# Another order of the work around cells 3 and 4 and the first weight pieces, in an mLSTM cell with an act-GCU feed-forward

## The chip, the cores and the metric

The kernel runs on one core of one Trainium2 chip. The time is device microseconds of that core, the median of several executions. A profile is one more execution, recorded by the hardware profiler.

## The reference

An mLSTM cell is run over four batches, eight heads, 768 time steps and 40 dimensions. Its output, as 3072 rows of 320, goes through a feed-forward block with a cosine gate.

```python
for t in range(S):                                   # S = 768
    m_new = max(f_gate[t] + m, i_gate[t])
    f_stab, i_stab = exp(f_gate[t] + m - m_new), exp(i_gate[t] - m_new)
    m = m_new
    C = f_stab * C + i_stab * outer(v[t], k[t])      # 40 x 40 for each head
    n = f_stab * n + i_stab * k[t]
    y[t] = sigmoid(o_gate[t]) * (C @ q[t]) / max(abs(n @ q[t]), 1)
x = y as (3072, 320)
h = x @ w_in                                         # 320 -> 2048
out = (h * cos(h)) @ w_out                           # 2048 -> 320
```

The two weight matrices arrive as float64 and are turned into float32 on the chip.

## The kernel before

Time is cut into six chunks of 128 steps. A *cell* is one chunk of one batch with its eight heads, numbered n = 4 * chunk + batch, so there are 24. Within a cell the recurrence becomes matrices: scores (k against q, `scores`, L492), times a decay matrix E (`weigh`, L498), times v (`values`, L508 for the first four cells, L518 to L527 later, where the state from earlier chunks is added with the scaled q, qG). The output is divided by a denominator and gated by sigmoid(o): `normalize` for cells 0 to 3, `denominators` and `divide` for later ones. `seam` holds cell n's last matmuls: for cells 0 to 3 the transposes of y into xT (px, L610 and L612), and for all the state's increment (pu, L619). `seam_out` brings the last dimensions into xL, for cells from 4 on by two DMAs issued on ScalarE's queue (L626). `state` adds the increment, `fade` decays the state before.

E is built from running maxima of the gates that go through DRAM (M_d), are loaded as broadcasts (L369), masked on GpSimd (`decay_exponents`, an affine select, L399) and exponentiated on ScalarE (`decay`, L413). The gates of chunk 0 are handled first; those of chunks 1 to 5 ("later gates") are worked out beside cells 0 to 3, then transposed on TensorE into a table (`gates_turn`, L275, with a product of a diagonal, L276) and copied to `tab` by ScalarE (`gates_keep`, L281 and L282).

The feed-forward of a chunk is done in eight steps f2, each with two 128-column blocks of w_in. `Up(c, f2)` issues the up-projection into two PSUM banks (tag "up", two banks in all): four 128x512 products with w_in_sb (L667) and two for the last 64 rows of x with w_in_l (L661). Then come `near` on ScalarE (rounding, L675), `rest` on VectorE (L678), `sin` on ScalarE (L683) and `gate` on VectorE (L687), which frees the banks. `down` multiplies by w_out (L699), in the first chunk one step behind: `down_slot(0, f2)` issues `down(0, f2 - 1)`.

The order of each engine's instructions is the order in which the code issues them (a manual schedule): `first_cells` (cells 0 to 3), `first_period` (cell 4 with chunk 0's steps 0 and 1), then `both_parts(c, b)`, two steps f2 = 2b and 2b + 1 with cell 4(c + 1) + b between them. TensorE's clock is kept up in the head by `warm`, matmuls on zeros (L920).

Weights come in pieces. `weights_in(f)` loads three pieces for the steps 2f and 2f + 1: two of w_in_sb (four DMAs each, L141) and one of w_in_l (four DMAs, L179). `weights_out(p)` loads the piece of w_out for step p (one DMA of 640 KB, L185). A piece is converted by `take_apart` (two operations on ScalarE, L153 and L155), `bound` (two on VectorE, L159 and L160) and `put_together` (one on VectorE, L166, and one on GpSimd, L167). The raw pieces lie in pools: `pb` has four buffers, for input pieces and also for cell 3's E; `pc` has three, for output pieces. `load_out(p)` loads output piece p + 3 as soon as piece p is converted. Nearly all loads are issued on SP's queue, in program order, each after the load before it on its semaphore has landed; a load whose buffer isn't free yet holds all loads behind it.

`clear_low` sets to zero the second set of buffers for q and k in blocks (GpSimd, L448), `turn_blocks` transposes q and k in 32x32 blocks on VectorE (L465), `turn_gate` the gate o (L470), `scale_q` and `weigh_k` are GpSimd products (L474, L418), `odd_values` a GpSimd copy of parts of v (L424). `sin_next` runs a sine on one element, so that ScalarE's table is loaded ahead of the next `sin`.

Of the kernel before, what the change touches and what calls it, by code (L numbers as in the profile page):

```python
# [29 lines left out]
def kernel(  # L30
# [239 lines left out]
    def gates_turn():  # L270
        pg = ps_o.tile([128, R, 2, BH], FP, name="pg", tag="o")
        pd = ps_o.tile([128, R - 1, BH], FP, name="pd", tag="o")
        for c in range(R):
            for j, src in enumerate((a1, eW)):
                nc.tensor.transpose(pg[:, c, j], src[:, c], ident[0:BH, 0:BH])  # L275
        nc.tensor.matmul(pd.rearrange("p c b -> p (c b)"), one.to_broadcast([BH, 128]), dd.rearrange("r c b -> r (c b)"),  # L276
                         start=True, stop=True)
        return pg, pd

    def gates_keep(pg, pd):  # L280
        nc.scalar.copy(out=tab[:, 1:NC, 0:2], in_=pg)  # L281
        nc.scalar.copy(out=tab[:, 1:R, 3], in_=pd)  # L282
# [261 lines left out]
    def divide(n):  # L544
        c, b = divmod(n, B)
        vt, dn = heads_of[n], dns[n]
        yt = p1.tile([128, 3, C], FP, name="yt", tag="yt")
        nc.vector.tensor_tensor(out=yt, in0=vt, in1=oTs[n], op=OP.mult)
        nc.vector.reciprocal(out=dn, in_=dn)
        db = p1.tile([128, 3, C], FP, name="db", tag="db")  # L550
        for i, mask in enumerate(([FROM0] * 32, [FROM1] * 32, [FROM0] * 16 + [FROM1] * 16)):
            nc.vector.stream_shuffle(out=db[:, i], in_=dn, mask=mask)
        if b == 0:
            new_x(c)

        nc.vector.tensor_tensor(out=xT[c][:, NK * b:NK * b + NK + 1], in0=yt, in1=db, op=OP.mult)
        ys[n] = xT[c][:, NK * b + NK]
# [364 lines left out]
    def first_cells():  # L922
        nc.vector.memset(nil, 0.0)
        gates_in()
        nc.scalar.copy(out=ident_b, in_=ident)
        load(0, "qk")
        later_gates_in()
        load(0, "v")
        load(1, "qk")
        load_o(0, (0, 1))  # L930
        load(1, "v")
        load(2, "qk")
        load_E(0)
        load_E(1)
        warm(12)
        wall_in(0, 0, pmu)
        wall_in(0, 1, psum_o())
        gates_first()
        gates_first_out()
        spread(0, 0)  # L940
        decay_exponents_half(0, 0)
        turn(0)
        turn_out(0, False)
        gates_sums()
        spread(0, 1)
        decay_exponents_half(0, 1)
        decay(0)
        weigh_k(0)
        load_E(2)
        load(2, "v")  # L950
        load_E(3)
        load_o(0, (2, 3))
        load(3)
        pieces.extend(weights_in(0))
        wall_in(1, 0, psum_o())
        wall_in(1, 1, psum_o())
        gates_less_sums()
        spread(1, 0)
        decay_exponents_half(1, 0)
        scores(0)  # L960
        gates_maxima()
        turn(1)
        weigh(0)
        sigmoid(0, slice(0, 2))
        turn_out(1, False)
        spread(1, 1)
        decay_exponents_half(1, 1)
        gates_exponents()
        decay(1)
        weigh_k(1)  # L970
        values(0)
        normalize(0)
        scores(1)
        gates_exp()
        turn(2)
        turn_out(2, False)
        warm(2)
        seam(0)
        weigh(1)
        seam_out(0)  # L980
        state(0)
        load_two(B, "qk")
        decay_exponents(2)
        gates_diagonal()
        decay(2)
        weigh_k(2)
        values(1)
        load_M(B)
        outs.append((0, weights_out(0)))
        normalize(1)  # L990
        scores(2)
        turn(3)
        sigmoid(0, slice(2, 4))
        seam(1)
        weigh(2)
        decay_exponents(3)
        turn_out(3)
        seam_out(1)
        values(2)
        decay(3)  # L1000
        weigh_k(3)
        state(1)
        normalize(2)
        scores(3)
        pg = gates_turn()
        warm(1)
        seam(2)
        weigh(3)
        to_float32(*pieces.pop(0))
        seam_out(2)  # L1010
        state(2)
        for piece in pieces[0:2]:
            take_apart(*piece)
        gates_keep(*pg)
        values(3)
        more = weights_in(1)
        pieces.append(next(more))
        load_G(B)
        load_two(B, "Kv")
        normalize(3)  # L1020
        bound(pieces[0][0])
        put_together(*pieces.pop(0))
        warm(3)
        seam(3)
        decay_exponents(B)
        seam_out(3)
        bound(pieces[0][0])
        put_together(*pieces.pop(0))
        pieces.extend(more)
        load_M(B + 1)  # L1030
        outs.append((1, weights_out(1)))
        load_o(1)
        outs.append((2, weights_out(2)))
        load_E(B + 2)
        low_dimensions(B)
        turn_blocks(B)
        state(3)
        decay(B)
        weigh_k(B)
        odd_values(B)  # L1040
        scale_q(B)

    spot = const.tile([1, 1], FP, name="spot")
    nc.gpsimd.memset(spot, 0.0)
# [14 lines left out]
    def first_period():  # L1059
        n = B  # L1060
        up = Up(0, 0)
        scores(n)
        warm(8, psum_o())
        for e in range(2):
            up.near(e)
        for e in range(2):
            up.rest(e)
        weigh(n)
        for e in range(2):
            up.sin(e)  # L1070
            up.gate(e)
        values(n)
        seam(n)
        p, piece = outs.pop(0)
        take_apart(*piece)
        take_apart(*pieces[0])
        bound(piece[0])
        put_together(*piece)
        load_out(p)
        bound(pieces[0][0])  # L1080
        put_together(*pieces.pop(0))
        decay_exponents(n + 1)
        denominators(n)
        for piece in pieces:
            take_apart(*piece)
        turn_blocks(n + 1, "k")
        up = Up(0, 1)
        for dst, bits in pieces:
            bound(dst)
            put_together(dst, bits)  # L1090
        pieces.clear()
        for e in range(2):
            up.near(e)
        for e in range(2):
            up.rest(e)
        for e in range(2):
            up.sin(e)
            up.gate(e)
        clear_low()
        fade(n)  # L1100
        down_slot(0, 1)
        sigmoid(1)
        turn_blocks(n + 1, "q")
        turn_gate(n)
        state(n)
        divide(n)
        decay(n + 1)
        p = next_out()
        seam_out(n)
        scale_q(n + 1)  # L1110
        weigh_k(n + 1)
        sin_next()
        pieces.extend(weights_in(2))
        load_two(n + 2)
        load_E(n + 3)
        load_out(p)

    def both_parts(c, b):

# [2 lines left out]
        for i in range(2):  # L1122
# [11 lines left out]
            if i == 0:  # L1134
                if cell:
                    weigh(n)
                    if n + 1 < N:
                        decay_exponents(n + 1)
                for e in range(2):
                    up.sin(e)  # L1140
                    up.gate(e)
                if c > 0:
                    sums(c, f2)
                if b == 0 and c == 1:
                    sigmoid(c + 1)

                if c == 0:
                    made = [pieces.pop(0) for _ in range(min(1, len(pieces)))]
                    p, piece = outs.pop(0)
                    made.append(piece)  # L1150
                    for dst, bits in made:
                        take_apart(dst, bits)
                    for dst, bits in made:
                        bound(dst)
                    for dst, bits in made:
                        put_together(dst, bits)
                    load_out(p)
                if cell and n + 1 < N:
                    decay(n + 1)
            else:  # L1160
                if cell:
                    seam_out(n)
                if cell:
                    state(n)
                for e in range(2):
                    up.sin(e)
                    up.gate(e)
                if c > 0:
                    sums(c, f2)
                if n == B + 1:  # L1170
                    low_dimensions(n + 1)
                if pieces:
                    to_float32(*pieces.pop(0))
                if cell and n + 1 < N:
                    if c > 0:
                        weigh_k(n + 1)
                    odd_values(n + 1)
# [84 lines left out]
```

## Time and profile before

| | us |
|---|---|
| median of 3 runs | 533.39 |
| lowest, highest | 532.88, 535.65 |
| the profiled execution | 535.21 |
| its span | 533.4 |
| TensorE busy | 516.5 (97%) |
| VectorE, ScalarE, GpSimd busy | 422.8, 285.5, 226.2 |
| mean granted TensorE clock | 0.981 |

The span runs from the first to the last instruction that the profile shows; 1.8 us lie around it. Times in the parts below count from the start of the span. A busy engine is one with an instruction in it; TensorE at half clock counts as busy all the same, so its busy time is read together with the granted clock.

### The profile page before, as it was taken

The page shows a single profiled execution, that of the slowest core. Times are in us where ns is not written, and L with a number is a line of the kernel's source. Part 1 is how long each engine was busy: PE and PEld are TensorE (multiplying, and loading weights), DVE is VectorE, ACT ScalarE, POOL GpSimd, SP SyncE. Part 2 cuts the span into 40 slices and gives each one's busy share as a digit, 9 for nine tenths or more (in the row PEclk, how much of TensorE's full clock was granted, in tenths as well). Part 3 has the DMA queues.
Part 4 walks back from the last instruction along what each step waited for, and adds up shares of the span by engine and source line. Part 5 has one row for each costly group of instructions (what it writes and reads, how often), then busy time and mean ns, then how long its engine had stood idle before and what let it go on. Part 6 is the DMA issues. An engine that isn't in the chain of part 4 may idle for free.

```text
span 533.4 us, 10501 instructions
## 1 busy us (share of the span) xinstructions
PE 516.5 (97%) x3844; PEld 350.2 (66%) x3844; DVE 422.8 (79%) x908; ACT 285.5 (54%) x546; POOL 226.2 (42%) x369
## 2 busy tenths in 40 slices
PE   7999879999999999999999999999999999999997
PEld 4875436556667757667767667767657767575666
DVE  5867978997888878898878898878898878664645
ACT  2877597757566537826527826526836522232230
POOL 7524644554577572632632632642422421222211
PEclk9977979999999999999999999999999999999999
DMA  9969869978949449229149229159220000010001
GB/s 138 219 194 195 229 173 198 224 123 243 183 120 189 46 124 178 66 83 188 32 124 163 53 87 188 29 129 170 37 88 7 2 5 6 1 50 1 0 1 49
DMA packets 99939, 57.81 MB, mean 108 GB/s; under 512 B 62304, under 2 KB 92608, under 8 KB 99888
## 3 DMA queue, kind: packets, MB, share of 16 engines
q1 hardware_dynamic: 96352, 55.48, 48.6%
q10 hardware_dynamic: 3392, 1.49, 1.3%
q8 instruction: 30, 0.49, 0.4%
q14 instruction: 21, 0.17, 0.1%
q0 software_dynamic: 144, 0.18, 0.1%
HBM read 51.71 MB, written 4.11 MB: 105 GB/s over the span
## 4 chain that ended last, share of the span: by engine, by line
PE 81%; DVE 5%; DMA 5%; SPq 3%; ACT 3%; POOL 2%; issue 1%; DVEq 0%; POOLq 0%; ACTq 0%
PE pup L667 28%; PE acc L848 24%; PE pup L661 8%; PE po L699 5%; PE late L848 3%; PE ps L492 3%; PE vt L527 2%; PE vt L518 2%; DMA bits<-in_moe_w_in_dram 2%; DMA o<-in_o_gate_dram 2%; PE pu L619 1%; SPq L141 1%; SPq L329 1%; DVE t L465 1%; DMA bits<-in_moe_w_out_dram 1%
## 5 line engine op out<-in xcount | busy, mean ns | idle before, releaser
L667 PE MATMUL pup<-xT,w_in_sb 128*128 128x512 f32 x384 | 178.7, 609 | 2.3 <-POOL qr L448 2.0
L675 ACT ACTIVATE n<-pup 128x512 int32<-128x512 f32 x96 | 53.9, 594 | 187.6 <-PE pup L661 133.8
L667 PEld LDWEIGHTS pup<-xT,w_in_sb 128*128 128x128 f32 x384 | 71.2, 194 | 90.1 <-issue 84.5
L678 DVE SCALAR_TENSOR_TENSOR n<-pup,n 128x512 f32<-128x512 f32 x96 | 63.1, 687 | 70.0 <-ACT n L675 68.5
L741 POOL TENSOR_TENSOR D<-g 128x128 f32<-128x128 f32 x40 | 19.8, 495 | 214.2 <-DVE g L687 214.2
L683 ACT ACTIVATE n<-n 128x512 f32<-128x512 f32 x96 | 57.7, 627 | 26.6 <-DVE n L678 19.0
L687 DVE SCALAR_TENSOR_TENSOR g<-pup,n 128x512 f32<-128x512 f32 x96 | 61.7, 684 | 3.9 <-ACT n L683 3.3
L848 PE MATMUL acc<-w_out_sb,g 128*128 128x160 f32 x320 | 59.0, 306 | 0.0
L848 PE MATMUL acc<-T,g 128*128 128x160 f32 x304 | 55.0, 301 | 0.0
L661 PE MATMUL pup<-xL,w_in_l 64*128 64x512 f32 x192 | 54.2, 642 | 0.0
L848 PEld LDWEIGHTS acc<-w_out_sb,g 128*128 128x128 f32 x320 | 47.7, 190 | 8.7 <-issue 7.2
L413 ACT ACTIVATE E<-E,tab 128x128 f32<-128x128 f32 x160 | 49.0, 389 | 0.3
L848 PEld LDWEIGHTS acc<-T,g 128*128 128x128 f32 x304 | 45.9, 191 | 1.8 <-issue 1.4
L699 PE MATMUL po<-w_out_sb,g 128*128 128x320 f32 x128 | 37.9, 451 | 3.4 <-POOL w_out_sb L167 3.4
L699 PEld LDWEIGHTS po<-w_out_sb,g 128*128 128x128 f32 x128 | 24.9, 197 | 15.5 <-POOL w_out_sb L167 3.6
L848 PE MATMUL acc<-T,S 128*128 128x160 f32 x160 | 34.8, 300 | 0.0
L492 PEld LDWEIGHTS ps<-t,t 40*128 40x128 f32 (+1 forms) x384 | 24.7, 188 | 12.3 <-DVE t L465 6.2
L498 DVE TENSOR_TENSOR E<-ps,E 128x512 f32<-128x512 f32 x48 | 30.7, 680 | 0.0
L661 PEld LDWEIGHTS pup<-xL,w_in_l 64*128 64x128 f32 x192 | 14.5, 185 | 22.9 <-issue 21.2
L848 PE MATMUL acc<-w_out_sb,S 128*128 128x160 f32 x160 | 28.8, 300 | 0.0
L1048 ACT ACT_TABLE_LOAD x22 | 28.2, 1283 | 0.9 <-DVE w_out_sb L160 0.5
L492 PE MATMUL ps<-t,t 40*128 40x128 f32 (+1 forms) x384 | 26.3, 276 | 1.2 <-DVE t L465 1.2
(189 smaller groups left out, 882.0 us busy)
## 6 DMA issues: line engine op xcount, KB each, us to landing
E<-M_d SPq DMA_DIRECT2D x22, 512.0 KB
qr<-in_q_dram SPq DMA_DIRECT2D x36, 160.0 KB
kr<-in_k_dram SPq DMA_DIRECT2D x36, 160.0 KB
bits<-in_moe_w_out_dram SPq DMA_DIRECT2D x8, 640.0 KB
G<-G_d SPq DMA_DIRECT2D x20, 256.0 KB
bits<-in_moe_w_in_dram SPq DMA_DIRECT2D x32, 128.0 KB
out_dram<-o_sb SPq DMA_DIRECT2D x23, 160.0 KB
ks<-in_k_dram SPq DMA_DIRECT2D x10, 320.0 KB
```

The source lines that it names most:

```text
L413: nc.scalar.activation(out=Es[n][:, h], in_=Es[n][:, h], func=AF.Exp, scale=-1.0, bias=tab[:, c, 0, g:g + 1])
L492: nc.tensor.matmul(ps[j][:, p], kT[r, p], qT[r, p], start=True, stop=True)
L498: nc.vector.tensor_tensor(out=w, in0=pss[n][j], in1=w, op=OP.mult)
L661: nc.tensor.matmul(pu, w_in_l[r, f2], xL[c][r].rearrange("p b t -> p (b t)"), start=ahead, stop=not ahead)
L667: nc.tensor.matmul(pu.rearrange("p (b t) -> p b t", b=B), w_in_sb[:, i, ts(2 * f2 + e, 128)], xT[c][:, i:NK * B:NK], start=(i == 0 and not ...
L675: nc.scalar.activation(out=self.n[e], in_=self.pu[e], func=AF.Copy, bias=0.25)
L678: nc.vector.scalar_tensor_tensor(out=self.n[e].bitcast(FP), in0=self.pu[e], scalar=0.25, in1=self.n[e], op0=OP.add, op1=OP.subtract)
L683: nc.scalar.activation(out=r, in_=r, func=AF.Sin, scale=TWO_PI_DOWN)
L687: nc.vector.scalar_tensor_tensor(out=g, in0=self.pu[e], scalar=TWO_PI, in1=self.n[e].bitcast(FP), op0=OP.mult, op1=OP.mult)
L699: nc.tensor.matmul(po[c][b], gs[c, f][:, ts(b, C)], w_out_sb[:, f], start=(f == 0), stop=(f == NF - 1))
L848: nc.tensor.matmul(a, lhs, rhs, start=start, stop=stop)
L1048: nc.scalar.activation(out=spot, in_=spot, func=AF.Sin)
```

## The change

In `first_cells`, the later gates' transposes move from behind cell 3's scores to behind its values, and the warming matmuls with them: one became two ahead of cell 2's seam, three became two behind the transposes. The copy of the table moves behind cell 3's `seam_out`, and `scale_q(B)` goes ahead of `weigh_k` and `odd_values`.

In `first_period`, all three pieces of the second input weights are taken apart before anything else, and cell 4's values are copied from PSUM to SBUF on ScalarE (`out_of_psum`, new). The transpose of k moves behind the second step's `rest`. The second output piece is taken apart ahead of the sigmoid and put together ahead of cell 4's division; its successor (piece 4) is therefore loaded ahead of `weights_in(2)`. Denominators, fade, state, mask and the clearing stand ahead of that conversion. Cell 4's `seam_out` moves into `both_parts(0, 1)`, behind that step's sines, and the prepared sine goes. `divide` of cell 4 multiplies in place.

```diff
     def divide(n):
...
-        yt = p1.tile([128, 3, C], FP, name="yt", tag="yt")
+        yt = vt if n == B else p1.tile([128, 3, C], FP, name="yt", tag="yt")
...
         scores(3)
-        pg = gates_turn()
-        warm(1)
+        warm(2)
         seam(2)
         weigh(3)
...
             take_apart(*piece)
-        gates_keep(*pg)
         values(3)
+        pg = gates_turn()
+        warm(2)
         more = weights_in(1)
...
         put_together(*pieces.pop(0))
-        warm(3)
         seam(3)
+        seam_out(3)
         decay_exponents(B)
-        seam_out(3)
         bound(pieces[0][0])
         put_together(*pieces.pop(0))
+        gates_keep(*pg)
         pieces.extend(more)
...
         decay(B)
+        scale_q(B)
         weigh_k(B)
         odd_values(B)
-        scale_q(B)
...
     def first_period():
...
         seam(n)
         p, piece = outs.pop(0)
         take_apart(*piece)
-        take_apart(*pieces[0])
+        for some in pieces:
+            take_apart(*some)
+        out_of_psum(n)
         bound(piece[0])
         put_together(*piece)
         load_out(p)
-        bound(pieces[0][0])
-        put_together(*pieces.pop(0))
-        decay_exponents(n + 1)
-        denominators(n)
-        for piece in pieces:
-            take_apart(*piece)
-        turn_blocks(n + 1, "k")
         up = Up(0, 1)
         for dst, bits in pieces:
             bound(dst)
...
         for e in range(2):
             up.rest(e)
+        turn_blocks(n + 1, "k")
         for e in range(2):
             up.sin(e)
             up.gate(e)
+        p, piece = outs.pop(0)
+        take_apart(*piece)
+        denominators(n)
+        fade(n)
+        state(n)
+        decay_exponents(n + 1)
         clear_low()
-        fade(n)
+        turn_blocks(n + 1, "q")
+        bound(piece[0])
+        put_together(*piece)
+        load_out(p)
         down_slot(0, 1)
         sigmoid(1)
-        turn_blocks(n + 1, "q")
+        decay(n + 1)
         turn_gate(n)
-        state(n)
         divide(n)
-        decay(n + 1)
-        p = next_out()
-        seam_out(n)
         scale_q(n + 1)
         weigh_k(n + 1)
-        sin_next()
         pieces.extend(weights_in(2))
         load_two(n + 2)
         load_E(n + 3)
-        load_out(p)
+
+    def out_of_psum(n):
+        vt = p1.tile([128, 3, C], FP, name="vt_s", tag="yt")
+        nc.scalar.copy(out=vt, in_=heads_of[n])
+        heads_of[n] = vt
...
     def both_parts(c, b):
...
                     up.gate(e)
+                if (c, b) == (0, 1):
+                    seam_out(B)
                 if c > 0:
                     sums(c, f2)
```

## The prediction

> **What bounds the kernel now.** I read the page's busy times and its clock row first, then the table of busy times by stretches over the first 120 us, then the timeline where those stretches show idle or a low clock. In the table the columns are: stretch, its length, busy time of TensorE, its weight load, VectorE, ScalarE, GpSimd, then the granted clock, the DMA share and GB/s.
>
> ```profile
> PE 516.5 (97%) x3844; PEld 350.2 (66%) x3844; DVE 422.8 (79%) x908; ACT 285.5 (54%) x546; POOL 226.2 (42%) x369
> ...
> PEclk9977979999999999999999999999999999999999
> ```
> ```profile
> 32.00:36.00 4.00, 4.00 (x31) 3.13 (x31) 2.14 (x4) 2.69 (x9) 1.28 (x1) 0.50 0.84 254
> 36.00:40.00 4.00, 3.78 (x15) 2.59 (x15) 1.36 (x6) 2.20 (x6) 0.00 (x0) 0.50 0.33 115
> 40.00:45.70 5.70, 5.60 (x27) 3.12 (x28) 5.34 (x10) 4.11 (x14) 3.12 (x3) 0.50 1.03 208
> ...
> 62.70:66.10 3.40, 1.35 (x5) 0.55 (x4) 3.27 (x7) 2.11 (x3) 2.66 (x4) 1.00 0.95 343
> 66.10:69.60 3.50, 3.50 (x6) 1.48 (x5) 2.37 (x7) 3.46 (x7) 1.63 (x5) 0.51 1.03 262
> ...
> 73.00:76.40 3.40, 0.21 (x1) 0.21 (x2) 2.09 (x4) 2.61 (x6) 1.82 (x2) 1.00 0.37 106
> 76.40:79.80 3.40, 3.40 (x7) 2.12 (x7) 3.37 (x7) 3.40 (x6) 3.01 (x3) 0.50 0.29 98
> ...
> 98.60:120.00 21.40, 21.27 (x148) 12.78 (x150) 20.25 (x44) 15.21 (x29) 12.69 (x13) 1.00 0.79 149
> ```
>
> TensorE is the bound: from 98.6 us on it is busy 21.27 of 21.40 us at full clock. What the change can touch is the time before that: about 14 us at half clock from 32 us on, and two idle spells (62.7 to 66.1 and 73.0 to 76.4), each followed by some 3.4 us at half clock. So the question is how much earlier the steady part starts, which I read at one mark, cell 6's scores at 98.73 us. Everything behind that mark I leave as it is.
>
> **Part 1, the head.** These rows are start, length, engine, line and operation, and in brackets the idle time before with what ended it.
>
> ```profile
> 22.86 1.98 PE L508 MATMUL ph<-vs,E 128*128 128x41 f32 x16
> ...
> 29.72 1.16 PE L492 MATMUL ps<-t,t 64*128 64x128 f32 x16
> ...
> 30.83 0.56 DVE L576 TENSOR_TENSOR y<-yo,dn 128x256 f32<-128x256 f32 x2
> ...
> 31.96 0.75 PE L276 MATMUL pd<-dd,one 32*128 32x128 f32 x2 [0.34 <-ACT st L642]
> ...
> 33.03 0.64 PE L610 MATMUL px<-ident,y 128*128 128x128 f32 x2
> ...
> 34.86 3.64 PE L508 MATMUL ph<-vs,E 128*128 128x41 f32 x16
> ...
> 38.54 0.17 DVE L568 SCALAR_TENSOR_TENSOR dn<-ph,least 128x8 f32<-128x8 f32 x1 [4.29 <-PE ph L508]
> 38.57 1.73 SPq L141 DMA_DIRECT2D bits<-in_moe_w_in_dram x4
> ...
> 41.96 5.54 PE L667 MATMUL pup<-xT,w_in_sb 128*128 128x512 f32 x8
> ```
>
> Between cell 3's scores (end 30.88) and cell 2's seam (33.03) stand the gates' transposes, their product on L276 and one warming matmul, although the seam's input y is ready at 31.39. After the change only two warming matmuls stand there, so the seam starts at about 31.4. It and cell 3's values took 5.5 us here at half clock (33.03 to 38.50); the values alone took 1.98 us at full clock earlier. So the values end at 34.6 if the clock holds past 32 us, at 36.2 to 36.9 if it doesn't. I take 34.6, since the small 32-row transposes and the 0.34 us of idle go from just ahead of the drop.
>
> Two things hang on that end. VectorE waits 4.29 us for it, and SP's first load of the second input weights (38.57) waits for the buffer of cell 3's decay matrix, with all loads behind it. It goes up to 3.9 us earlier, but the two or three transfers then in flight have to finish. The DMA share of 0.33 from 36 to 40 leaves 2.7 us of empty engines to fill. I take 2.6 us earlier for every later landing (bounds 1 and 3.9).
>
> The transposes are not saved but put behind the values, where cell 3's normalization covers them (38.54 to 40.10 here). The later copy of the gate table on ScalarE costs nothing, since its reader comes after it in ScalarE's own order, and GpSimd's use of it waits for other data. The first up-projection then starts about 3.1 us behind the values, at 37.7. It took 6.5 us here, mostly at half clock, and 4.6 at full clock (first row of the next fence and the 1.13 us of L661). So its end lies between 42.3 and 44.2 and I take 43.0, set by the conversion of its last weights.
>
> **Part 2, the first period.**
>
> ```profile
> 93.43 3.60 PE L667 MATMUL pup<-xT,w_in_sb 128*128 128x512 f32 x8
> ```
> ```profile
> 48.58 1.09 ACT L675 ACTIVATE n<-pup 128x512 int32<-128x512 f32 x2 [1.82 <-PE pup L661]
> ...
> 50.86 0.30 POOL L424 COPY vr<-vs 128x128 f32<-128x128 f32 x1 [1.95 <-DMA vs<-in_v_dram]
> ...
> 51.21 0.43 PE L518 MATMUL vt<-E,vs 128*32 128x128 f32 x8
> ...
> 51.65 1.29 DVE L687 SCALAR_TENSOR_TENSOR g<-pup,n 128x512 f32<-128x512 f32 x2
> ...
> 52.44 0.43 PE L527 MATMUL vt<-qG,st 128*32 128x128 f32 x8 [0.80 <-POOL qG L474]
> ...
> 54.36 1.13 PE L661 MATMUL pup<-xL,w_in_l 64*128 64x512 f32 x4
> ...
> 58.95 4.47 PE L699 MATMUL po<-w_out_sb,g 128*128 128x320 f32 x16
> ...
> 64.63 1.29 DVE L687 SCALAR_TENSOR_TENSOR g<-pup,n 128x512 f32<-128x512 f32 x2
> ...
> 65.47 5.37 PE L667 MATMUL pup<-xT,w_in_sb 128*128 128x512 f32 x8 [2.05 <-POOL qr L448]
> ...
> 71.73 1.06 PE L492 MATMUL ps<-t,t 40*128 40x128 f32 x16
> ...
> 74.58 1.56 POOL L167 TENSOR_TENSOR w_out_sb<-w_out_sb,bits 128x640 int32<-128x640 int32 x1 [6.77 <-DVE w_out_sb L166]
> ...
> 76.19 6.27 PE L699 MATMUL po<-w_out_sb,g 128*128 128x320 f32 x16 [3.40 <-POOL w_out_sb L167]
> ...
> 82.39 0.43 PE L518 MATMUL vt<-E,vs 128*32 128x128 f32 x8
> ```
>
> Cell 4's values need v, which lands at 50.8 (the wait before L424) and so at 48.2 after: 3.0 us earlier than 51.21. The 0.80 us on qG goes, because the scaling of q no longer stands behind GpSimd's two waits for k and v. The second up-projection starts at 50.6 instead of 54.36. It and the down-projection behind it (4.47 us) end at 59.8.
>
> The 2.05 us before 65.47 is named for GpSimd, but what the third up-projection needs is a free bank, and VectorE's first gate, done 0.65 us after 64.63, gives it. That chain starts from ScalarE's 48.58, now 43.0 (5.5 us earlier), and loses the denominators; the transpose of k stays ahead of the gate but moves beside ScalarE's sine. The copy of cell 4's values out of PSUM (128x384) is new on ScalarE, under 0.6 us by the 0.54 of each 128x512 in the L675 row, and lies where ScalarE waits for the second up-projection. The gate comes at about 59, TensorE at 59.8: no idle, no lost clock. The third up-projection takes 4.7 us instead of 6.26 (65.47 to 71.73). Cell 5's scores start at 64.4: 7.3 us gained.
>
> The second down-projection waits for the second output weights. Their conversion stands behind sigmoid, decay and cell 4's division now, and ahead of them after. On VectorE it follows the denominators, the state and q's transpose and ends at 64.1; on GpSimd fade, mask and both clearings now come before it, while VectorE does that work, and the 1.56 us end it at 65.8. So the matmuls start at 65.8 instead of 76.19, at 4.47 instead of 6.27 us, and cell 5's values come at 70.3 instead of 82.39. At this point 12.1 us are gained: 3.0 + 0.8, then 1.9 of the first idle spell, 1.6 of clock, 3.1 of the second spell, 1.7 of clock.
>
> **Part 3, what is late next.** From the chain of waits, the timeline and SP's waits:
>
> ```profile
> 39.41 2.42 DMA bits<-in_moe_w_in_dram
> ```
> ```profile
> 77.48 0.66 ACT L153 ACTIVATE w_in_sb<-bits 128x512 f32<-128x512 f32 x1
> ...
> 83.56 1.57 POOL L167 TENSOR_TENSOR w_out_sb<-w_out_sb,bits 128x640 int32<-128x640 int32 x1
> ...
> 88.46 0.60 ACT L675 ACTIVATE n<-pup 128x512 int32<-128x512 f32 x1 [1.94 <-PE pup L667]
> ...
> 89.12 4.47 PE L699 MATMUL po<-w_out_sb,g 128*128 128x320 f32 x16
> ...
> 98.73 1.16 PE L492 MATMUL ps<-t,t 40*128 40x128 f32 x16 [0.64 <-DVE t L465]
> ```
> ```profile
> SPq L141 <- DMA xL<-xT: 2.8, 1, 2.8
> ```
>
> The fifth output piece's load moves ahead of the third input weights' in SP's queue, and it needs the buffer that the second piece's conversion frees at 65.8. All of SP waits behind it. At 262 GB/s its 640 KB and the 512 KB of the next piece take 4.4 us, with 2.42 from issue to landing: 72.7, and 75.1 if another 640 KB is still ahead. I take 73.5. ScalarE is there at about 71 and waits, where it started at 77.48 without a wait. On the other side, the division's result no longer holds SP (2.8 us) in this place, but a few loads later.
>
> From there on ScalarE's own chain sets the pace. It ran from 77.48 to 86.52 (88.46 less 1.94 of idle), so 73.5 leads to 82.6, and the third output weights, which GpSimd finished at 85.13, 7.7 us behind ScalarE's start, come at 81.2. TensorE is ready at 77.0 (6.7 us behind the values, as from 82.39 to 89.12) and waits 4.2 us; the down-projection goes at 81.2 instead of 89.12. From ScalarE's 88.46 to cell 6's scores at 98.73 it is 10.3 us, of which I take 10.2 to stay. So the scores start at 92.8: **5.9 us gained** at the mark, 6.2 given back. The profiled execution took 535.21 us for a span of 533.4; 535.21 - 5.9 = 529.3. It lies 1.8 above the median of 533.39, so against the median that is 4.1 us (0.8%).
>
> The clock row matters once more: a stretch with 1.35 busy of 3.40 us was followed by half clock, which costs 1.7 us. After the change I see gaps of 4.2 us from 77 on and of some 1.8 us ahead of cell 6's scores; a drop behind the first is hidden by ScalarE's chain, one behind the second is not. The Trainium skill ("TensorE: Matmul & The Clock Gate", Part 1) has the clock halved after an idle window of about 3.4 us, counted in free-running windows. By that rule the second gap would cost nothing, and the sum would stay 529.3; by the row it may become 531.0. The trace disagrees with the rule here, since 2.05 us sufficed.
>
> **Rivals.** About 0.5% (2.7 us) is what a measurement can tell from no change.
> - Nothing is late: the next input weights land by 71. For it: 0.37 and 0.29 of DMA share from 73 to 79.8, room that now fills earlier. Against: SP's new order. Of the 12.1 us some 9 stay: 526.2. Chance 0.13.
> - The transfers decide and hardly move: share 1.03 from 40 to 45.7 says that the queue is full where v comes, or the clock falls at 32 us all the same and the reordered head does not do its work. Then v lands near 50, the first gap stays, and the second one's gain is mostly given back in part 3: 2 us, 533.2. Chance 0.21.
> - Slower: the fifth output piece blocks SP. If the second piece's conversion on GpSimd ends no earlier than before (76.1, behind mask and clearings, with VectorE's share late), the next input weights land at 83.8, cell 6's scores start 19.3 us behind that at 103.1, and it takes 539.6. It decides from 74.4 on, 8.6 us later than I expect. Chance 0.14.
>
> **The numbers.** The forecast has 0.52, with its own range 527 to 531.5; about four fifths of it, the first rival and a trace of the second lie below 530.7: faster 0.56. The rest of the two middle cases is the same: 0.30. Slower 0.14. From 525 to 534.5 us leaves out the slower case and the ends of the others, together 0.2.
>
> **What would show it.** Right: values of cell 3 ending near 34.6 us, SP's load right behind; no idle before the third up-projection; the second down-projection near 66; ScalarE waiting on a DMA near 71 to 74; cell 6's scores near 93. Wrong: v still landing near 50; SP's load of the fifth output piece issued after 74; or scores of cell 6 beyond 96, with a cause in VectorE or in clock windows that I have not counted.

## The result, and the profile after

| | before | after |
|---|---|---|
| median, us (runs) | 533.36 (20) | 531.52 (20) |
| lowest, highest | 531.21, 535.71 | 530.34, 532.91 |
| ratio after / before, 95% interval | | 0.9967 (0.9952 to 0.9982) |
| the profiled execution | 535.21 | 532.28 |
| its span | 533.4 | 530.5 |
| mean granted TensorE clock in it | 0.981 | 0.987 |
| cell 6's scores, the mark | 98.73 | 95.46 |

The change makes the kernel 1.84 us (0.33%) faster. The forecast was 529.3, so 2.2 us are missing, and the result lies within the half per cent that the prediction called no change, though its interval excludes a ratio of 1. Between the two profiled executions the mark comes 3.3 us earlier, where 5.9 was expected.

First the page of after: engine totals, and the granted clock in 40 slices.

```profile
PE 512.6 (97%) x3844; PEld 348.6 (66%) x3844; DVE 426.3 (80%) x908; ACT 285.5 (54%) x546; POOL 227.9 (43%) x369
...
PEclk9988997999999999999999999999999999999999
```

Then the table of busy times by stretches (the columns are those of the prediction: stretch, length, the five engines, clock, DMA share, GB/s).

```profile
36.00:40.00 4.00, 4.00 (x28) 2.53 (x28) 3.59 (x6) 2.66 (x9) 2.38 (x2) 0.69 1.06 272
...
49.20:52.70 3.50, 3.45 (x72) 3.19 (x72) 3.43 (x5) 1.30 (x4) 2.54 (x2) 0.58 0.57 167
...
68.70:73.60 4.90, 4.54 (x16) 2.93 (x16) 4.79 (x13) 3.13 (x5) 3.83 (x3) 1.00 1.03 313
...
83.50:86.90 3.40, 3.35 (x6) 2.19 (x7) 3.30 (x10) 2.96 (x5) 2.07 (x5) 0.50 1.42 162
```

The long fall of the clock at 32 us is gone; what is left in the head is a short one (0.69 from 36 to 40). An idle spell of 3.6 us now stands ahead of cell 4's values and is followed by a low clock (0.58 from 49.2 to 52.7); in before, warming matmuls ran up to these values. The idle spell before the second down-projection is down from 3.4 us to 1.5. A new fall of the clock is seen at 83.5. The transfers run at a share near 1 and at 313 GB/s (68.7 to 73.6) just ahead of ScalarE's wait for the third input weights.

The timeline of after, with start, length, engine, line, operation, and the idle time before it with what ended it:

```profile
32.20 1.98 PE L508 MATMUL ph<-vs,E 128*128 128x41 f32 x16
...
34.25 2.38 SPq L141 DMA_DIRECT2D bits<-in_moe_w_in_dram  x4
...
49.17 0.86 POOL L424 COPY vr<-vs 128x128 f32<-128x128 f32 x1 [1.04 <-DMA vs<-in_v_dram]
...
49.25 0.66 PE L518 MATMUL vt<-E,vs 128*32 128x128 f32 x8 [3.62 <-ACT bits L155]
...
52.76 1.13 PE L661 MATMUL pup<-xL,w_in_l 64*128 64x512 f32 x4
...
60.60 1.19 POOL L448 MEMSET qr<- 128x1312 f32 x1
...
60.95 2.05 DVE L541 TENSOR_SCALAR dt<-vt_s 128x128 f32<-128x128 f32 x1
...
61.66 3.60 PE L667 MATMUL pup<-xT,w_in_sb 128*128 128x512 f32 x8
61.73 1.19 POOL L448 MEMSET kr<- 128x1312 f32 x1
...
62.53 6.48 SPq L185 DMA_DIRECT2D bits<-in_moe_w_out_dram  x2
...
67.05 1.56 POOL L167 TENSOR_TENSOR w_out_sb<-w_out_sb,bits 128x640 int32<-128x640 int32 x1 [4.13 <-ACT E L413]
...
68.67 4.58 PE L699 MATMUL po<-w_out_sb,g 128*128 128x320 f32 x16 [1.45 <-POOL w_out_sb L167]
...
69.07 8.35 SPq L141 DMA_DIRECT2D bits<-in_moe_w_in_dram  x8
...
73.64 0.42 PE L518 MATMUL vt<-E,vs 128*32 128x128 f32 x8 [0.40 <-ACT n L683]
...
76.50 0.66 ACT L153 ACTIVATE w_in_sb<-bits 128x512 f32<-128x512 f32 x1 [2.95 <-DMA bits<-in_moe_w_in_dram]
...
80.23 1.75 POOL L167 TENSOR_TENSOR w_in_sb<-w_in_sb,bits 128x512 int32<-128x512 int32 x1 [7.70 <-DVE w_in_sb L166]
...
81.47 0.27 DVE L541 TENSOR_SCALAR dt<-vt 128x128 f32<-128x128 f32 x1
...
83.55 7.58 PE L699 MATMUL po<-w_out_sb,g 128*128 128x320 f32 x16 [2.94 <-POOL w_out_sb L167]
...
90.97 3.60 PE L667 MATMUL pup<-xT,w_in_sb 128*128 128x512 f32 x8
...
95.46 1.14 PE L492 MATMUL ps<-t,t 40*128 40x128 f32 x16
...
96.53 4.57 PE L699 MATMUL po<-w_out_sb,g 128*128 128x320 f32 x16
```

Read down the list, each row against its forecast. Cell 3's values end at 34.18 (34.6 expected), with SP's load right behind. Cell 4's values start at 49.25 (48.2). The second up-projection starts at 52.76 (50.6), the third at 61.66 (59.8), and no idle stands before it, as expected. The conversion of the second output piece ends at 68.61 (65.8). Cell 5's values come at 73.64 (70.3; 82.39 before). ScalarE does wait for the third input weights, but until 76.50 (73.5). The third down-projection starts at 83.55 (81.2), the mark is at 95.46 (92.8). The order of events is the one forecast; from cell 4's values on, the steps come 1.1 to 3.3 us late.

### The profile page after: what moved, and what is told of

Its sections match the earlier page's. It is cut to its first block, busy times and chain, and to the rows that moved or that the text cites. A ratio compares the mean times of both kernels' runs of the same rounds, so it can differ in the third digit from the quotient of the medians.

```text
span 530.5 us, 10499 instructions
## 1 busy us (share of the span) xinstructions
PE 512.6 (97%) x3844; PEld 348.6 (66%) x3844; DVE 426.3 (80%) x908; ACT 285.5 (54%) x546; POOL 227.9 (43%) x369
## 4 chain that ended last, share of the span: by engine, by line
PE 79%; DVE 8%; DMA 5%; POOL 2%; ACT 2%; SPq 1%; issue 1%; DVEq 0%; POOLq 0%; ACTq 0%
PE pup L667 27%; PE acc L848 24%; PE pup L661 8%; PE po L699 4%; PE late L848 3%; PE ps L492 3%; PE vt L527 2%; PE vt L518 2%; DMA bits<-in_moe_w_out_dram 2%; DMA G<-G_d 2%; PE pu L619 1%; PE ph L508 1%; DMA bits<-in_moe_w_in_dram 1%; PE pw L920 1%; DVE g L687 1%
## 5 line engine op out<-in xcount | busy, mean ns | idle before, releaser
L667 PE MATMUL pup<-xT,w_in_sb 128*128 128x512 f32 x384 | 175.4, 600 | 0.2
L699 PE MATMUL po<-w_out_sb,g 128*128 128x320 f32 x128 | 39.3, 464 | 4.4 <-POOL w_out_sb L167 4.4
L474 POOL TENSOR_TENSOR qG<-t,G 128x512 f32<-128x512 f32 x20 | 25.7, 1283 | 8.8 <-DVE E L498 4.3
L848 PEld LDWEIGHTS acc<-T,S 128*128 128x128 f32 x160 | 26.3, 191 | 1.4 <-issue 1.4
```

The lines of the kernel that those rows point to most:

```text
L474: nc.gpsimd.tensor_tensor(out=qG, in0=qkT[n][0], in1=Gs[n], op=OP.mult)
L667: nc.tensor.matmul(pu.rearrange("p (b t) -> p b t", b=B), w_in_sb[:, i, ts(2 * f2 + e, 128)], xT[c][:, i:NK * B:NK], start=(i == 0 and not ...
L699: nc.tensor.matmul(po[c][b], gs[c, f][:, ts(b, C)], w_out_sb[:, f], start=(f == 0), stop=(f == NF - 1))
L848: nc.tensor.matmul(a, lhs, rhs, start=start, stop=stop)
```

## The experiments

All are compared with the kernel before, run on the same chip beside them. The theory after the result was: the order of the matmuls does what it should, but two things on other engines take the gain back, the 640 KB of output piece 4 ahead of the third input weights, and the clearing ahead of the conversion of the second output piece. The rival was that TensorE's own path in the head, the wait for v and the clock that it loses there, takes it.

| kernel | median, us (runs) | ratio, 95% interval | mark, us |
|---|---|---|---|
| after | 531.52 (20) | 0.9967 (0.9952 to 0.9982) | 95.46 |
| head_only | 532.02 (12) | 0.9961 (0.9936 to 0.9986) | 95.70 |
| period_only | 532.92 (12) | 0.9994 (0.9965 to 1.0023) | 96.35 |
| late_load | 529.91 (12) | 0.9932 (0.9902 to 0.9962) | 93.88 |
| late_clear | 530.17 (12) | 0.9951 (0.9923 to 0.9978) | 94.15 |
| both_late | 528.83 (8) | 0.9915 (0.9883 to 0.9947) | 93.70 |
| v_first | 533.27 (12) | 0.9987 (0.9964 to 1.0011) | 95.78 |
| warm22 | 531.22 (12) | 0.9959 (0.9934 to 0.9985) | 94.56 |
| all_three | 530.45 (12) | 0.9929 (0.9903 to 0.9954) | 93.80 |
| period_late | 530.97 (12) | 0.9970 (0.9942 to 0.9999) | 93.77 |
| four_bufs | 530.73 (1) | - | 94.88 |
| out_first | 529.95 (6) | 0.9930 (0.9907 to 0.9954) | 93.13 |
| late_out_first | 528.81 (6) | 0.9906 (0.9882 to 0.9929) | 90.92 |

The mark is that of one profiled execution, whose clock can differ from the median's, so the medians decide and the marks explain. The interval of late_load overlaps after's a little, late_clear's widely; of the 12 executions of each, seven took less than the fastest of after's 20 (530.34).

**The two halves of the change.** head_only is the kernel before with the new `first_cells`; period_only is the changed kernel with the old `first_cells`.

> The old first period behind the new head. If the changed kernel's gain comes from the head (cell 3's values end near 34.2 us instead of 38.5, the second up-projection starts about 1.6 us earlier, at 52.8), the time falls about 1.5 us against the kernel before (near 532). If the head only moves work that a later wait gives back, because the third up-projection waits for VectorE and the second down-projection for the second output weights as before, it stays within 0.5 us.

> The old head with the new first period. If the new order in the first period carries the gain, the idle spells before the third up-projection and the second down-projection (2.05 and 3.40 us) shrink to under 2 us together and the time falls 1 to 2 us against the kernel before, ahead of what the third input weights give back. If the gain needs the earlier head, the third input weights, which then land later than 76 us, take all of it back: no change, or up to 1 us slower.

head_only gains 1.3 us against 533.34 on its chip, period_only 0.4 with an interval that holds no change. In head_only's timeline both idle spells of the first period are still there:

```profile
62.45 5.37 PE L667 MATMUL pup<-xT,w_in_sb 128*128 128x512 f32 x8 [2.28 <-POOL qr L448]
...
73.16 2.52 PE L699 MATMUL po<-w_out_sb,g 128*128 128x320 f32 x5 [3.39 <-POOL w_out_sb L167]
```

In period_only's they are gone, but ScalarE then waits for the third input weights, as in after:

```profile
77.44 0.67 ACT L153 ACTIVATE w_in_sb<-bits 128x512 f32<-128x512 f32 x1 [2.17 <-DMA bits<-in_moe_w_in_dram]
```

So the new first period removes some 5.5 us of idle TensorE time (2.28 and 3.39, less 0.21 that is left) and brings next to nothing by itself: its gain is given back behind it. Much of the head's gain lies in the spread of the executions. Of the 35 executions of before on this chip, 14 took 535.2 us or more, all at a mean granted clock of 0.976 to 0.981; none of head_only's 12 took more than 532.79, at 0.987 or above, and none of after's 20 more than 532.91. The profile of before, with its fall of the clock at 32 us, is of one of those 14. In period_only's profile, with the same old head, the fall is absent, and the mean clock (0.985 or above) suggests the same for the other 21, whose median of 532.53 is only 0.5 above head_only's. That all 14 have their low clock at 32 us was not seen.

**Piece 4's load behind the other loads.** late_load:

```diff
         put_together(*piece)
-        load_out(p)
         down_slot(0, 1)
...
         load_two(n + 2)
         load_E(n + 3)
+        load_out(p)
```

> The changed kernel with the load of output piece 4 put back behind the loads of the third input weights. Theory of the queue: piece 4's load waits for the second output piece's conversion (68.6 us) and holds the input weights behind it; without that they are issued from 63 us on, land near 72 to 73, ScalarE's wait of 2.95 us and TensorE's 2.94 us go, and cell 6's scores come at 92 to 93 instead of 95.5: 2 to 3 us faster than the changed kernel. Rival, the transfers: the engines are full from 64 to 77 us whatever the order, the weights land within 1 us of 76, and the time stays within 0.7 us of the changed kernel.

It takes 529.91 us. The timeline:

```profile
61.16 2.44 DVE L541 TENSOR_SCALAR dt<-vt_s 128x128 f32<-128x128 f32 x1
...
62.52 11.05 SPq L141 DMA_DIRECT2D bits<-in_moe_w_in_dram  x8
...
74.89 0.71 ACT L153 ACTIVATE w_in_sb<-bits 128x512 f32<-128x512 f32 x1 [0.73 <-DMA bits<-in_moe_w_in_dram]
...
82.00 4.57 PE L699 MATMUL po<-w_out_sb,g 128*128 128x320 f32 x16 [0.79 <-POOL w_out_sb L167]
...
87.76 3.67 PE L667 MATMUL pup<-xT,w_in_sb 128*128 128x512 f32 x8 [1.19 <-DVE g L687]
...
93.88 1.16 PE L492 MATMUL ps<-t,t 40*128 40x128 f32 x16 [1.39 <-DVE t L465]
```

ScalarE's wait falls from 2.95 to 0.73 us, TensorE's before the third down-projection from 2.94 to 0.79; no half clock follows it, and it takes 4.57 us instead of 7.58. The mark and the median both come 1.6 us earlier. The profiled execution, at 532.07 the slowest of the 12, ends only 0.2 us before after's all the same. Behind TensorE's wait of 1.39 us ahead of the mark the clock falls again, and the down-projection behind the mark takes 6.26 us, where it took 4.57 in after without such a wait:

```profile
94.97 6.26 PE L699 MATMUL po<-w_out_sb,g 128*128 128x320 f32 x16
```

The prediction had said of this second gap that a fall behind it would not be hidden. In the profiles of late_clear, both_late and all_three it falls there too (6.26 or 6.27 us); in those of period_only, warm22, period_late and late_out_first the wait is as long (1.37 to 1.39 us) and it doesn't.

**The clearing behind the conversion.** late_clear:

```diff
-        clear_low()
         turn_blocks(n + 1, "q")
         bound(piece[0])
         put_together(*piece)
+        clear_low()
```

> The changed kernel with the clearing of the second q and k buffers behind the second output piece's conversion on GpSimd. If the clearing is what held VectorE's first denominator step (2.05 us instead of 0.28), that step falls to 0.3, the conversion ends near 66.5 instead of 68.6, the load of piece 4 and the input weights behind it come about 1.7 us earlier, and it is 1 to 1.7 us faster than the changed kernel. If something else held the step, or the transfers bind, nothing moves by more than 0.5 us.

It takes 530.17 us. The timeline:

```profile
62.69 0.21 DVE L541 TENSOR_SCALAR dt<-vt_s 128x128 f32<-128x128 f32 x1
...
66.98 1.57 POOL L167 TENSOR_TENSOR w_out_sb<-w_out_sb,bits 128x640 int32<-128x640 int32 x1 [6.14 <-issue]
...
68.88 4.58 PE L699 MATMUL po<-w_out_sb,g 128*128 128x320 f32 x16
```

The denominators' first step takes 0.21 us once GpSimd clears nothing beside it, against 2.05. The conversion ends at 68.55, about as in after, but v came late in this execution and the second up-projection started at 54.44; from there to the second down-projection it is 14.4 us, against 15.9 in after (68.67 - 52.76), and TensorE does not wait. The median is 1.35 us below after's. How the shorter step reaches the end is not shown by this trace: with the conversion ending as in after, the third input weights still come 1.26 us earlier (75.24), as did SP's load of output piece 3 (61.28 against 62.53), which lies ahead of the clearing.

**Both.** both_late has both edits.

> Both edits of before together: the load of piece 4 behind the third input weights, and the clearing behind the second output piece's conversion. If the conversion's end matters only because SP's queue hangs on it, the second edit adds nothing to the first: as fast as with the late load alone (529.9). If TensorE's wait for the second output weights (2.16 us with the late load) counts by itself, it falls to under 0.5 us and the two add up: near 528.5 to 529.

528.83 us: 2.7 below after, nearly the sum of 1.6 and 1.35, and 4.2 below before (533.0 on that chip). Its interval (0.9883 to 0.9947) doesn't touch after's, but overlaps those of late_load and late_clear. Its timeline has the second up-projection and the mark at:

```profile
53.09 1.62 PE L661 MATMUL pup<-xL,w_in_l 64*128 64x512 f32 x4
...
93.70 1.16 PE L492 MATMUL ps<-t,t 40*128 40x128 f32 x16 [1.36 <-DVE t L465]
...
94.79 6.27 PE L699 MATMUL po<-w_out_sb,g 128*128 128x320 f32 x16
```

The up-projection is even later than in after (52.76), and the mark 1.76 earlier.

**TensorE's path in the head.** v_first loads cell 4's k and v ahead of the second input weights; warm22 has 22 warming matmuls instead of 8 before cell 4's values; all_three is both_late with v_first.

```diff
+        load_two(B, "Kv")
         more = weights_in(1)
         pieces.append(next(more))
         load_G(B)
-        load_two(B, "Kv")
```
```diff
-        warm(8, psum_o())
+        warm(22, psum_o())
```

> The changed kernel with k and v of cells 4 and 5 loaded ahead of the second input weights and of G, so that they no longer queue behind cell 3's values. Theory of the queue: v lands near 45 instead of 49.1, TensorE's idle 3.62 us ahead of cell 4's values closes, and the second up-projection comes 3 us earlier; but what follows hangs on the second output piece's conversion and on the third input weights, so the time stays within 0.7 us of the changed kernel. If TensorE's path in the head counts to the end, it is 2 to 3 us faster than the changed kernel.

> The changed kernel with 22 warming matmuls instead of 8 ahead of cell 4's values, so that TensorE is busy on zeros in the 3.62 us in which it waits for v. If clock drops in the head cost what they seem to, the half clock behind that wait (3.4 us at 0.5) goes, cell 4's values take 0.43 instead of 0.69 us a group, and up to 1 us is gained at the second up-projection; at the end of the program I expect no more than 0.5 us of it. If the clock in the head counts fully it is 1.5 us faster.

> Late load, late clearing and k and v first together. If, once the third input weights no longer hang on the conversion, TensorE's own path from the head decides, it is 1 to 2 us faster than the first two together (under 528). If ScalarE's and VectorE's chain behind the third input weights decides, as in the forecast, it equals the first two together within 0.5 us.

v_first misses. The timeline:

```profile
46.54 0.42 PE L518 MATMUL vt<-E,vs 128*32 128x128 f32 x8
...
47.45 1.28 POOL L474 TENSOR_TENSOR qG<-t,G 128x512 f32<-128x512 f32 x1 [5.34 <-DMA G<-G_d]
...
49.92 0.56 POOL L424 COPY vr<-vs 128x128 f32<-128x128 f32 x1
...
52.77 2.08 PE L661 MATMUL pup<-xL,w_in_l 64*128 64x512 f32 x4
```

The values start 2.7 us earlier, but then need qG, whose G now comes behind v, and vr, which waits in GpSimd's order; the second up-projection starts where it did (52.77 against 52.76), and the kernel is 1.75 us slower than after. Why it is so much, when the mark is only 0.3 us later, its trace doesn't show. With both late edits it costs too: all_three 530.45 against 528.83. In warm22 the clock in the head stays at 1.00 from 48 to 52 us and the second up-projection starts at 51.66, 1.1 us earlier, but the median is only 0.3 below after's, with the intervals nearly the same. The timeline, and the table of stretches with a fall of the clock later:

```profile
51.66 1.13 PE L661 MATMUL pup<-xL,w_in_l 64*128 64x512 f32 x4
```
```profile
66.00:68.20 2.20, 0.34 (x4) 0.23 (x2) 2.17 (x3) 2.20 (x8) 1.85 (x2) 0.99 1.02 255
68.20:71.60 3.40, 3.40 (x7) 2.15 (x7) 3.29 (x11) 1.92 (x3) 3.40 (x3) 0.50 0.97 329
```

So a second up-projection 1.1 us earlier brings no gain that is clear of noise, and the rival theory finds no support: TensorE waits 1.85 us for the second output weights instead, and the clock falls behind that. v_first doesn't test it, since its up-projection is not earlier.

**The old head with the better period.** period_late is both_late with the old `first_cells`.

> The old head with the new first period, and in it the load of piece 4 behind the third input weights and the clearing behind the conversion. If the new first period alone was worth nothing because its own load order took its gain back, it now gains 2 to 3 us against the kernel before (530 to 531). If it needs the earlier head, it stays within 0.7 us of the kernel before.

530.97 us, 2.1 above both_late, with intervals that overlap slightly: with the period mended, the new head still seems worth its 1.3 us or more. Five of the 12 executions took 533.8 us or more, at a clock of 0.979 to 0.983; of both_late's eight none took more than 531.88, at 0.986 or above. That the low clock of those five lies in the head was not seen: the profiled one is not among them.

**What of the load costs, its wait or its bytes.** In four_bufs the pool of raw output pieces has four buffers instead of three, so that piece 4's load needn't wait for the conversion; two other pools have one buffer less each, to make room.

```diff
-    pc = ctx.enter_context(tc.tile_pool(name="pc", bufs=3))
+    pc = ctx.enter_context(tc.tile_pool(name="pc", bufs=4))
...
-    p3 = ctx.enter_context(tc.tile_pool(name="p3", bufs=3))
+    p3 = ctx.enter_context(tc.tile_pool(name="p3", bufs=2))
...
-    gp = ctx.enter_context(tc.tile_pool(name="gp", bufs=6))
+    gp = ctx.enter_context(tc.tile_pool(name="gp", bufs=5))
```

> The changed kernel with four buffers instead of three for the output pieces, paid for with one buffer less for the rounded values and one less for the gates, so only the trace up to cell 6's scores is read. The load of piece 4 keeps its place ahead of the third input weights but no longer waits for a buffer. If the wait in SP's queue is the loss, the load goes near 63 instead of 68.6, and the input weights land at 75 or before, 1.3 us or more earlier than 76.4. If the 640 KB ahead of them are the loss, they land within 0.5 us of 76.4 all the same.

```profile
61.85 1.10 SPq L185 DMA_DIRECT2D bits<-in_moe_w_out_dram  x2
...
63.01 13.76 SPq L141 DMA_DIRECT2D bits<-in_moe_w_in_dram  x8
...
75.95 0.67 ACT L153 ACTIVATE w_in_sb<-bits 128x512 f32<-128x512 f32 x1 [2.42 <-DMA bits<-in_moe_w_in_dram]
```

SP is free 5.4 us earlier (two issues in 1.10 us instead of 6.48) and starts the input weights' loads 6.1 us earlier, yet ScalarE has them only 0.55 us earlier, since they lie behind the same bytes. SP's wait for the buffer costs at most about half a microsecond, since the queue was 0.68 us ahead in this execution even before the wait (piece 3's load at 61.85, in after at 62.53). The bytes of piece 4 cost the rest of the 1.6, or some 1.0 if late_load's own lead (61.93) is taken off. These are single executions, so the split is rough.

**The order in which the late pieces are converted.** In out_first, `both_parts(0, b)` converts the output piece, which has long landed, ahead of the input piece that ScalarE waits for. late_out_first has this and both late edits.

```diff
-                    made.append(piece)
+                    made.insert(0, piece)
```

> The changed kernel, but in the first chunk ScalarE, VectorE and GpSimd convert the output piece ahead of the input piece. If ScalarE's wait for the third input weights is what holds the third output piece behind it, TensorE's 2.94 us ahead of the third down-projection go, with the clock drop behind them, and it is 1 to 2 us faster than the changed kernel (near 530). If the chain behind the input weights (second piece, rounding, cell 6's transposes) decides, cell 6's scores stay at 95 to 96 and the time within 0.5 us of 531.5.

> Late load, late clearing and the output piece first. If TensorE's 2.33 us ahead of the third down-projection count, another 0.5 to 1 us comes off (near 528). If the chain behind the input weights decides, it equals the first two alone (528.8) within 0.5 us.

out_first takes 529.95 us, 1.6 below after. late_out_first takes 528.81, no less than both_late, although its mark is the earliest of all:

```profile
78.17 4.47 PE L699 MATMUL po<-w_out_sb,g 128*128 128x320 f32 x16
84.81 3.67 PE L667 MATMUL pup<-xT,w_in_sb 128*128 128x512 f32 x8 [2.17 <-DVE g L687]
...
90.92 1.16 PE L492 MATMUL ps<-t,t 40*128 40x128 f32 x16 [1.39 <-DVE t L465]
```

The third down-projection starts 5.4 us earlier than in after and without a wait, and TensorE then waits 2.17 and 1.39 us for VectorE. What keeps its median at both_late's is open: the profiled execution, the fastest of six, had a mean clock of 0.994, both_late's, the slowest of eight, 0.986, so the two marks can't be compared closely. both_late and late_out_first are the versions that beat both kernels most, 4.2 to 4.5 us below before.

## Why the prediction was wrong in size

**The order of events was right.** Cell 3's values, SP's load behind them, the idle spell before the third up-projection gone, the second down-projection released by the earlier conversion, ScalarE waiting on a DMA: each is in the trace of after, and late_load shows by its median that the wait on that DMA reaches the end of the kernel.

**The sum, in the two profiled executions.** The term that failed is the landing of the third input weights, from which the forecast counts on to the mark. It was put at 73.5, and ScalarE had them at 76.50. From there to the mark the forecast has 19.3 us (73.5 to 92.8) and the run 18.96 (76.50 to 95.46): 3.00 - 0.34 = 2.66, which is all that is missing at the mark. In the ten kernels that have the new first period and convert the pieces in its order, the mark comes 18.9 to 19.2 us behind ScalarE's start on these weights. Cell 5's values do not set it: in late_load they come 0.6 us later than in after (74.25), and the mark 1.58 us earlier. The steps that lie behind this:

**Step 1, v and the second up-projection.** "I take 2.6 us earlier for every later landing": v came 1.7 earlier (the copies on L424 start at 49.17 and 50.86), and behind the idle spell that this leaves ahead of it, which I had not priced, the clock fell: a group of eight matmuls of the values took 0.66 us instead of 0.43. Together the second up-projection came 2.16 us late. On TensorE this cost little: warm22 takes back 1.1 of it for 0.3 us of median. In SP's queue the lead shrank further, to 0.4 us at the load of output piece 2 (60.24 against 60.63) and 0.3 at piece 3's (62.53 against this row of before), just ahead of the third input weights:

```profile
62.82 0.54 SPq L185 DMA_DIRECT2D bits<-in_moe_w_out_dram  x1
```

**Step 2, the conversion at 65.8.** It ended at 68.61. I had it "while VectorE does that work", with GpSimd's clearing beside VectorE's denominators at no price. That cover failed: L541 took 2.05 us and ended with the second clearing (63.00 and 62.92). It accounts for some 1.8 of the 2.8 us (2.05 against 0.21); the rest came with the late up-projection. The price could be read in the profile of before, where L160, a step of the same kind on SBUF, took 1.33 us beside a GpSimd conversion (L159, of the same size, took 0.28 just ahead of it, at 61.22):

```profile
61.44 1.29 POOL L167 TENSOR_TENSOR w_in_sb<-w_in_sb,bits 128x512 int32<-128x512 int32 x1 [1.14 <-DMA o<-in_o_gate_dram]
61.54 1.33 DVE L160 TENSOR_SCALAR w_in_l<-w_in_l 128x256 int32<-128x256 int32 x1
```

The copy of the values to SBUF seems to be what made it possible: of 20 such steps in the trace of after, the 19 that read PSUM took 0.26 to 0.29 us, one of them (81.47) while a GpSimd conversion ran (80.23 to 81.98). No run has the step on PSUM beside a clearing. The clearing moved away, in late_clear, brings 1.35 us of median, by a path that stays open. The Trainium skill ("SBUF — State Buffer", Who interferes with whom) says that a `tensor_scalar` can enter a mode which takes the port pair shared with GpSimd, and that the loser then waits for the whole instruction; the rows agree, with 0.21 us alone and 2.05 beside two clearings.

**Step 3, the third input weights at 73.5.** They came at 76.50. I had 7.7 us from the conversion's end to the landing, and 7.9 is what it was, but that is luck. four_bufs takes the conversion out of that chain and the landing moves by 0.55 us, no more than its queue was ahead already (0.68). What counts more is the traffic ahead, which runs at 313 GB/s and a share of 1.03; with piece 4 behind, ScalarE had the weights at 74.89. The prediction counted piece 4's bytes from the end of the hold at 65.8, and took piece 3's to have landed by then ("75.1 if another 640 KB is still ahead"). With the 2.6 us of step 1, piece 3's load would have gone at 60.2 (62.82 - 2.6); it went at 62.53. So the sum started from the wrong wait, SP's for the buffer, and put the loads ahead of these weights too early. How the 3.0 us split between the queue and the late conversion was not run by itself.

**Step 4, the clock behind the third gap.** The prediction held that a fall there is hidden by ScalarE's chain, and it was. After 2.94 us of idle the clock was at half for 6.8 us and the down-projection took 7.58 us. TensorE came out of it at 91.1 with the next up-projection at once. In late_load, without the fall, TensorE waits 1.19 us there for VectorE's gate and 1.39 us ahead of the mark for cell 6's transposes, and from the third input weights to the mark it is 18.99 us (74.89 to 93.88), as with the fall (18.96; both_late and four_bufs, which have a fall there too, 19.04 and 18.93). So this fall is no part of the miss. The Trainium skill ("TensorE: Matmul & The Clock Gate", Part 1) has an idle window of about 3.4 us before the clock falls; this gap is another one below it.

**The forecast against the run.** 529.3 was 535.21 less 5.9. The steps above miss 2.66 at the mark, 0.34 comes behind it (436.48 from the mark to the end in before, 436.82 in after), and the profiled execution of after is 0.76 above its median: 2.66 + 0.34 - 0.76 = 2.24, which is the miss of 2.2. The change against the median was forecast as 4.1 us and is 1.84. both_late, with piece 4's load and the clearing both moved back, gains 4.2.

**The rivals.** "The transfers decide and hardly move" comes nearest in time, but not as it was put: v did move, and the first gap went. Its full queue, though, fits the lead that shrank to 0.3 us. The slower case, piece 4 blocking SP, has its mechanism in the trace (SP holds for 5.4 us), but far below its point of 74.4; the hold itself is worth at most about 0.5.

## What to carry to other kernels

When an edit moves a load ahead in a queue, price two things apart: how long the queue stands still, and how many bytes now go ahead of what the next stage waits for; here, with the DMA share near 1, the bytes counted for more. A lead at the head of a queue need not last: 1.7 us at v were 0.3 a few loads later. "Hidden beside another engine" is a claim about both engines, and a copy of an operand from PSUM to SBUF may change who disturbs whom. And before a stretch of low clock in one profile is taken as a cost to be saved, look at the spread of the other executions and their mean clock: here, by their mean clocks, that stretch was in some of them only.

## What the runs showed of the hardware

- A VectorE step of 128x128 on SBUF took 0.20 to 0.22 us with GpSimd not clearing (late_clear, both_late, late_out_first, all_three, period_late), 0.74 to 2.44 us where it met one or two GpSimd clearings of 1.19 us (2.05 in after, 2.44 in late_load). In out_first, where it started 0.07 us ahead of the first clearing, it took 0.27, and the clearing 1.33; in late_load it started 0.04 us ahead, and took the 2.44. One of 128x256 took 1.33 beside a GpSimd conversion of 1.29 (before, 61.54).
- Gaps of 2.0 to 3.6 us of TensorE were often followed by 3.4 or 6.8 us at half clock, not always: 2.94 in after by 6.8, 2.33 in both_late (before 81.69) by 3.4, 2.00 in late_clear (before 82.28) by none. Of the eight waits of 1.36 to 1.39 us ahead of cell 6's scores, four were followed by half clock (late_load, late_clear, both_late, all_three).
- Executions of one kernel differed by several us in steps that go with the mean granted clock: the 35 executions of before beside head_only lie at 530.8 to 531.9 us (clock 0.990 to 0.997), 532.5 to 533.6 (0.985 to 0.992) and 535.2 to 538.1 (0.976 to 0.981).
